# One table load at the start of a fused attention and feed-forward kernel: a set that holds both exponential and logarithm

## The chip, the cores and the metric

The kernel runs on one core of a Trainium2 chip. The metric is the device time of one execution in microseconds. Of the unchanged kernel three timed runs are there, 1183.91 to 1187.83 us with a median of 1184.35, and one more execution that the hardware profiler recorded.

The core's engines are named as in the profile: PE (TensorE, matrix products), PEld (its weight loads), DVE (VectorE), ACT (ScalarE), POOL (GpSimd) and SP (SyncE, which issues DMAs here). Each engine works through its own queue in order and waits there for what the others produce.

## The reference

Two blocks stand one behind the other. The first normalises q and k by their root mean square, takes softmax attention for 8 batches of 12 heads (448 positions, 64 wide) and hands its output, as 3584 rows of 768, to the second: a product with `w_in`, `h` times its softmax, a layer norm without bias, and a product with `w_out`.

```python
def rmsnorm(x, g):
    rms = np.sqrt(np.mean(x * x, axis=-1, keepdims=True) + 1e-06)
    return x / rms * g
q_n, k_n = rmsnorm(q, g_q), rmsnorm(k, g_k)
scores = 1.0 / np.sqrt(64) * np.matmul(q_n, k_n.transpose(0, 1, 3, 2))
attn = np.exp(scores - np.max(scores, axis=-1, keepdims=True))
attn = attn / (np.sum(attn, axis=-1, keepdims=True) + 1e-09)
x = np.matmul(attn, v).transpose(0, 2, 1, 3).reshape(3584, 768)

h = x @ w_in                                   # 768 -> 1024
e = np.exp(h - np.max(h, axis=-1, keepdims=True))
solu = h * e / (np.sum(e, axis=-1, keepdims=True) + 1e-09)
mu, var = mean and variance of solu along the row
return ((solu - mu) / np.sqrt(var + 1e-06) * g_ln) @ w_out
```

`w_in` and `w_out` arrive as 64-bit floats, the other inputs as 32-bit ones: the kernel reads the two weights as pairs of 32-bit words and builds 32-bit floats from them.

## The kernel before

The work of the attention is cut into 48 pairs of heads (`pair(n)`, lines 640 to 653). For a pair, `load` (471) brings q, k and v; there are three q/k buffers, so the load of pair n + 3 needs the buffer of pair n, which is free when `qk_transpose(n)` has read it. `norm` (482) makes the inverse root mean squares; `qk_transpose` (507) turns q and k on PE; `scores` (520), called for four chunks of k, multiplies, takes the exponential (L531) and adds up the chunks on POOL (L535); `values` (537) multiplies with v, sums the exponentials on PE into `sm`, inverts them on DVE (L557 to L559) and writes a part of `xT` (L562).

`norm` is where the logarithm is. ScalarE squares (L485), DVE sums (L488), ScalarE takes Ln (L492) and then the Exp of minus one half of it (L494), which gives a first guess of the inverse root; DVE mends it with one Newton step (L493, L495 to L497), and POOL applies it to q (L500).

The feed-forward works on 28 tiles of 128 rows: `ff_in` (574, two halves of six products into `h`), `ff_solu` (585: the maximum on DVE, the exponential at L593 on ScalarE, statistics on DVE, a power on POOL), `ff_transpose` (607) and `ff_out` (617, two halves of eight products, a copy on ScalarE, a store). Its pieces are put between the pieces of the pairs: a tile may begin when the pairs it needs are through, and at most 4 pieces go with one pair (`RATE`, lines 681 to 704). What is left at the end follows behind the last pair.

The weights are converted in 28 steps between the pieces as well (`convert_w`, 444): `w_in` spread over the first 12 pairs, `w_out` over pairs 12 to 23. A step is five instructions on DVE, two on ScalarE (L452, L454) and the product on POOL or DVE (L459, L462).

The order in which each engine's instructions stand is not the order of these calls alone: the framework's scheduler moves instructions of one queue past one another where no data forbids it. In the trace the square of the second pair, for example, stands ahead of the first pair's L494.

ScalarE's functions are Square, Copy, Relu, Ln and Exp. The program says nothing of tables; the ACT_TABLE_LOAD instructions in the trace were put in when it was compiled.

`setup` (415) is called behind the first `load` and ahead of the first `norm`; it fills constants, makes the identity and turns the gains. The kernel has a second path for large gains (`general_path`, behind a condition at L753) that these inputs don't take.

Of the kernel before, what the change touches and what calls it, by code (L numbers as in the profile page):

```python
# [366 lines left out]
def fast_path(  # L367
# [16 lines left out]
    nc = tc.nc  # L384
# [28 lines left out]
    eps = consts.tile([P, 1], FP32, name="eps")  # L413

    def setup():
        nc.gpsimd.memset(mhalf, -0.5)
        nc.gpsimd.memset(m896, -896.0)
        nc.gpsimd.memset(eps, 1e-6)
        nc.gpsimd.memset(ones, 1.0)
        make_identity(nc, ident)  # L420
        pg = ps_t.tile([P, KF + 2], FP32, tag="t", name="pg")
        nc.tensor.transpose(pg, grow, ident[0 : KF + 2, 0 : KF + 2])
        nc.vector.tensor_copy(gcol, pg)  # L423

        nc.vector.tensor_scalar(
            gcol[:, KF : KF + 1], gcol[:, KF : KF + 1], gcol[:, KF + 1 : KF + 2], within, OP.mult, OP.mult
        )
# [226 lines left out]

    load(0)
    setup()
    load(1)
    norm(0)
# [126 lines left out]
```

## Time and profile before

| | |
|---|---|
| timed runs | 1183.91, 1184.35, 1187.83 us; median 1184.35 |
| profiled execution, its own time | 1183.37 us |
| its span, first to last instruction | 1181.6 us |
| mean granted PE clock | 0.965 of full |
| busy: PE, ACT, DVE, POOL | 1062.1, 533.1, 518.3, 392.5 us |

The profile is one execution. Busy times are sums over the span, and the span has stretches of different make: attention and weight conversion first, then attention and feed-forward mixed, then feed-forward alone. A row of a group reads: line, engine, operation, how many, then busy microseconds and the mean nanoseconds of one, then the idle time of the engine ahead of them and what ended it. The chain of waits is followed back from the last instruction: each step to what released it.

### The profile page before, as it was taken

The page shows a single profiled execution, that of the slowest core. Times are in us where ns is not written, and L with a number is a line of the kernel's source. Part 1 is how long each engine was busy: PE and PEld are TensorE (multiplying, and loading weights), DVE is VectorE, ACT ScalarE, POOL GpSimd, SP SyncE. Part 2 cuts the span into 40 slices and gives each one's busy share as a digit, 9 for nine tenths or more (in the row PEclk, how much of TensorE's full clock was granted, in tenths as well). Part 3 has the DMA queues.
Part 4 walks back from the last instruction along what each step waited for, and adds up shares of the span by engine and source line. Part 5 has one row for each costly group of instructions (what it writes and reads, how often), then busy time and mean ns, then how long its engine had stood idle before and what let it go on. Part 6 is the DMA issues. An engine that isn't in the chain of part 4 may idle for free.

```text
span 1181.6 us, 10970 instructions
## 1 busy us (share of the span) xinstructions
PE 1062.1 (90%) x3905; PEld 483.6 (41%) x3905; DVE 518.3 (44%) x922; ACT 533.1 (45%) x869; POOL 392.5 (33%) x242
## 2 busy tenths in 40 slices
PE   3667887997677999999999999999999999999997
PEld 1222333342223444444444444444444444455554
DVE  3896445578777344334233434334233433311300
ACT  6666786347776654434343435433343423110111
POOL 2756656144555532223232322223232322200000
PEclk9687999999977999999999999999999999999999
DMA  6521222013332111111111111111111100000001
GB/s 179 152 62 42 67 57 75 22 49 83 94 87 74 47 53 38 37 45 37 37 37 38 44 33 37 37 45 37 38 37 37 38 1 14 14 14 26 14 28 42
DMA packets 109047, 57.50 MB, mean 49 GB/s; under 512 B 91056, under 2 KB 101816, under 8 KB 108984
## 3 DMA queue, kind: packets, MB, share of 16 engines
q1 hardware_dynamic: 104640, 45.63, 15.0%
q10 hardware_dynamic: 4344, 11.08, 2.4%
q8 instruction: 33, 0.54, 0.2%
q14 instruction: 30, 0.25, 0.1%
HBM read 45.68 MB, written 11.01 MB: 48 GB/s over the span
## 4 chain that ended last, share of the span: by engine, by line
PE 68%; DVE 11%; ACT 11%; DMA 4%; issue 2%; SPq 2%; POOL 1%; ACTq 0%; DVEq 0%; POOLq 0%
PE po L624 25%; PE h L581 23%; PE s L527 9%; PE o L547 7%; DMA qk<-in_k_dram 3%; ACT E L531 3%; PE pt L514 2%; ACT L494 2%; PE sm L553 2%; SPq L479 2%; ACT sq L485 2%; DVE rs L488 1%; PE pu L614 1%; ACT L492 1%; DVE tmp L450 1%
## 5 line engine op out<-in xcount | busy, mean ns | idle before, releaser
L531 ACT ACTIVATE E<-s,rs 112x448 f32<-112x448 f32 x384 | 221.7, 633 | 243.6 <-PE s L527 241.1
L581 PE MATMUL h<-w_in,xT 128*128 128x512 f32 x672 | 312.1, 611 | 18.5 <-DVE xT L562 13.0
L624 PE MATMUL po<-w_out,uT 128*128 128x384 f32 x896 | 301.3, 491 | 6.8 <-ACT uT L615 6.2
L535 POOL TENSOR_TENSOR es<-es,E 112x896 f32<-112x896 f32 x96 | 203.3, 2118 | 256.5 <-ACT E L531 256.1
L527 PE MATMUL s<-qkT 64*112 64x448 f32 x768 | 195.5, 609 | 29.3 <-DVE qkT L518 19.4
L624 PEld LDWEIGHTS po<-w_out,uT 128*128 128x128 f32 x896 | 166.3, 190 | 135.6 <-ACT uT L615 14.4
L581 PEld LDWEIGHTS h<-w_in,xT 128*128 128x128 f32 x672 | 124.3, 193 | 172.9 <-issue 156.5
L535 POOL TENSOR_TENSOR es<-E 112x896 f32<-112x896 f32 x48 | 101.8, 2122 | 261.6 <-ACT E L531 261.6
L547 PE MATMUL o<-E,v 112*64 112x448 f32 x768 | 161.2, 561 | 0.0
L527 PEld LDWEIGHTS s<-qkT 64*112 64x112 f32 x768 | 63.0, 184 | 146.2 <-issue 109.3
L625 ACT COPY y<-po 128x384 f32<-128x384 f32 x56 | 26.6, 476 | 200.1 <-PE po L624 200.1
L488 DVE TENSOR_REDUCE rs<-sq 112x16 f32<-112x1024 f32 x48 | 58.4, 1217 | 109.4 <-ACT sq L485 109.0
L590 DVE TENSOR_REDUCE hmax<-h 128x1 f32<-128x1024 f32 x28 | 34.2, 1222 | 162.5 <-PE h L581 162.4
L547 PEld LDWEIGHTS o<-E,v 112*64 112x64 f32 x768 | 52.6, 141 | 107.7 <-issue 89.8
L485 ACT ACTIVATE sq<-qk 112x1024 f32<-112x1024 f32 x48 | 50.7, 1057 | 79.3 <-DMA qk<-in_k_dram 79.1
L500 POOL TENSOR_TENSOR qn<-qk,rs 112x512 f32<-112x512 f32 x48 | 55.8, 1162 | 85.1 <-PE pt L514 59.7
L514 PE MATMUL pt<-ident,qn 112*128 112x112 f32 x192 | 30.4, 284 | 49.5 <-DVE r L557 17.0
L518 DVE TENSOR_SCALAR qkT<-pt,gcol 128x448 f32<-128x448 f32 x48 | 32.6, 678 | 92.0 <-PE pt L514 92.0
L557 DVE STREAM_TRANSPOSE r<-sm 128x448 f32<-128x448 f32 x48 | 30.9, 643 | 83.1 <-PE sm L553 83.1
L492 ACT ACT_TABLE_LOAD x48 | 61.6, 1283 | 4.6 <-DVE gcol L423 3.8
L494 ACT ACT_TABLE_LOAD x43 | 55.2, 1283 | 0.8
L495 DVE TENSOR_TENSOR nx<-nx,ny 112x16 f32<-112x16 f32 x48 | 18.1, 377 | 81.4 <-ACT ny L494 81.4
(57 smaller groups left out, 747.8 us busy)
## 6 DMA issues: line engine op xcount, KB each, us to landing
qk<-in_q_dram SPq DMA_DIRECT2D x96, 112.0 KB, 2.9
qk<-in_k_dram SPq DMA_DIRECT2D x96, 112.0 KB, 3.0
v<-in_v_dram SPq DMA_DIRECT2D x48, 224.0 KB, 2.6
out_dram<-y ACTq DMA_DIRECT2D x28, 384.0 KB, 2.3
raw<-in_moe_w_in_dram SPq DMA_DIRECT2D x12, 512.0 KB, 4.9
raw<-in_moe_w_out_dram SPq DMA_DIRECT2D x16, 384.0 KB, 3.2
grow<-in_g_q_dram ACTq DMA_DIRECT2D x2, 0.2 KB
grow<-in_g_k_dram ACTq DMA_DIRECT2D x2, 0.2 KB
```

The source lines that it names most:

```text
L485: nc.scalar.activation(sq, d["qk"].rearrange("p s j h d -> p (s j h) d"), AF.Square)
L488: nc.vector.tensor_reduce(flat, sq, AX, OP.add)
L492: nc.scalar.activation(y, flat, AF.Ln, scale=1.0 / D, bias=eps[0:SP])
L494: nc.scalar.activation(y, y, AF.Exp, scale=-0.5)
L500: nc.gpsimd.tensor_tensor(d["qn"], d["qk"][:, 0].rearrange("p j h d -> p (j h) d"), rs[:, 0].rearrange("p j h -> p (j h) ()").to_broadcast ...
L514: nc.tensor.transpose(pt[:, j * SP : (j + 1) * SP], src, ident[0:SP, 0:SP])
L527: nc.tensor.matmul(s, d["qkT"][hh, 1, kc * SP : (kc + 1) * SP], d["qkT"][hh, 0, :], start=True, stop=True)
L531: nc.scalar.activation(d["E"][:, kc, h], d["s", h], AF.Exp, scale=d["rs"][:, 1, kc, h : h + 1])
L535: nc.gpsimd.tensor_tensor(d["es"], d["E"][:, 0] if kc == 1 else d["es"], d["E"][:, kc], OP.add)
L547: nc.tensor.matmul(o[h * D : (h + 1) * D, :], d["v"][:, h, kc * D : (kc + 1) * D], d["E"][:, kc, h], start=(kc == 0), stop=(kc == NJ - 1),)
L581: nc.tensor.matmul(d["h"][:, hs], xTs[m][:, c, i * P : (i + 1) * P], w_in[:, c, hs], start=(c == 0), stop=(c == KD - 1))
L624: nc.tensor.matmul(po, d["uT"][:, c], w_out[:, c, hs], start=(c == 0), stop=(c == KF - 1))
```

## The change

One instruction is added at the head of `setup`: a load of the activation table set with number 6, which holds both the exponential and the logarithm. Nothing else in the program is changed; where other loads stand is, as before, decided when it is compiled.

```diff
@@ -413,6 +413,12 @@
     eps = consts.tile([P, 1], FP32, name="eps")
 
     def setup():
+
+        nc.scalar.add_instruction(
+            mybir.InstLoadActFuncSet(
+                act_func_set_id=6, name=nc.get_next_instruction_name(), engine=mybir.EngineType.Activation
+            )
+        )
         nc.gpsimd.memset(mhalf, -0.5)
         nc.gpsimd.memset(m896, -896.0)
         nc.gpsimd.memset(eps, 1e-6)
```

## The prediction

> **What bounds the kernel now.** I read the page's totals first, then ScalarE's instructions grouped by line, then busy time by stretch of the span, then the waits and the chain that ended last, and at the end one turn of that chain in order of time.
>
> ```profile
> span 1181.6 us, 10970 instructions
> PE 1062.1 (90%) x3905; PEld 483.6 (41%) x3905; DVE 518.3 (44%) x922; ACT 533.1 (45%) x869; POOL 392.5 (33%) x242
> L492 ACT ACT_TABLE_LOAD x48 | 61.6, 1283 | 4.6 <-DVE gcol L423 3.8
> L494 ACT ACT_TABLE_LOAD x43 | 55.2, 1283 | 0.8
> ...
> L531 ACT ACT_TABLE_LOAD x5 | 6.4, 1283 | 0.1
> L485 ACT ACT_TABLE_LOAD x1 | 1.3, 1283 | 5.3 <-DMA qk<-in_k_dram 5.3
> ```
>
> TensorE (PE) is busy 90% of the span, ScalarE (ACT) 45%. ScalarE loads a table 48 + 43 + 5 + 1 = 97 times, 1.283 us each: 124.5 us (61.6 + 55.2 + 6.4 + 1.3), 23% of its busy time. One load stands before each of the 48 Ln (L492) and one before what follows it, the Exp of L494 or, 5 times, the scores' Exp of L531. Whether those 124.5 us set the time depends on the stretch:
>
> ```profile
> core 0: us, PE busy (x) PEld busy (x) DVE busy (x) ACT busy (x) POOL busy (x), PEclk, DMA share, GB/s
> 0.00:25.00 25.00, 6.98 (x23) 3.56 (x23) 8.37 (x26) 15.80 (x21) 4.01 (x13) 1.00 0.64 148
> 25.00:105.00 80.00, 49.14 (x185) 18.75 (x184) 68.56 (x103) 55.64 (x91) 54.95 (x31) 0.77 0.37 108
> 105.00:203.00 98.00, 78.60 (x378) 31.84 (x378) 42.24 (x88) 72.42 (x116) 58.26 (x33) 0.97 0.25 62
> 203.00:250.00 47.00, 44.19 (x124) 18.12 (x124) 30.37 (x55) 18.92 (x31) 13.97 (x10) 0.96 0.14 38
> 250.00:400.00 150.00, 117.74 (x496) 46.19 (x496) 109.21 (x192) 101.22 (x169) 77.62 (x42) 0.89 0.30 78
> 400.00:450.00 50.00, 48.59 (x186) 22.56 (x184) 18.79 (x34) 26.43 (x42) 15.17 (x10) 1.00 0.15 44
> 450.00:1026.00 576.00, 570.41 (x2060) 262.16 (x2058) 209.80 (x373) 223.84 (x370) 163.72 (x101) 1.00 0.12 34
> ```
>
> From 450 us on PE is busy 570.41 of 576.00 us: what ScalarE does there is hidden, and after 1026 us there are no loads. Before 400 us PE has gaps, and there the loads can count. The chain that ended last holds 30 whole loads between these two, the first and the last of them, and none behind 450 us:
>
> ```profile
> 13.95 1.28 ACT L494
> ...
> 426.89 1.28 ACT L494
> ```
>
> By stretch the 30 are 4 before 25 us, 6 from 25 to 105, 11 from 105 to 203, none from 203 to 250, 7 from 250 to 400 and 2 from 400 to 450. One turn of the chain, out of the steady part of the third stretch (start, duration, engine, line; in brackets the idle time before):
>
> ```profile
> 159.69 1.06 ACT L485 ACTIVATE sq<-qk 112x1024 f32<-112x1024 f32 x1
> 160.76 1.28 ACT L492 ACT_TABLE_LOAD   x1
> 160.84 1.22 DVE L488 TENSOR_REDUCE rs<-sq 112x16 f32<-112x1024 f32 x1 [4.70 <-ACT sq L485]
> 161.89 1.76 PE L527 MATMUL s<-qkT 64*112 64x448 f32 x8
> 162.10 0.31 ACT L492 ACTIVATE ny<-rs,eps 112x16 f32<-112x16 f32 x1
> 162.42 1.28 ACT L494 ACT_TABLE_LOAD   x1
> 163.72 0.21 ACT L494 ACTIVATE ny<-ny 112x16 f32<-112x16 f32 x1
> 163.84 2.19 ACT L531 ACTIVATE E<-s,rs 112x448 f32<-112x448 f32 x4
> 163.96 0.18 DVE L495 TENSOR_TENSOR nx<-nx,ny 112x16 f32<-112x16 f32 x1 [1.69 <-ACT ny L494]
> 164.06 0.64 DVE L557 STREAM_TRANSPOSE r<-sm 128x448 f32<-128x448 f32 x1
> 164.75 0.60 PE L514 MATMUL pt<-ident,qn 112*128 112x112 f32 x4 [1.10 <-DVE nx L496]
> 165.89 1.23 SPq L479 DMA_DIRECT2D qk<-in_q_dram  x2
> 167.16 1.28 SPq L479 DMA_DIRECT2D qk<-in_k_dram  x2
> 171.40 1.06 ACT L485 ACTIVATE sq<-qk 112x1024 f32<-112x1024 f32 x1 [0.74 <-DMA qk<-in_k_dram]
> ```
>
> This is a loop of 171.40 - 159.69 = 11.71 us per pair: square, sum on VectorE (DVE), Ln, load, Exp, then DVE's queue (L495 waits for Exp, and L557, which reads the `sm` bank so that PE can have it back, stands behind L495), the transposes, the four DMA issues that reuse the q/k buffer, their landing, the next square. Two loads stand in it, and they are not worth the same.
>
> **The change part by part.** *One load added in setup.* It stands on ScalarE behind the DMA issues of lines 740 to 745 and replaces the load at L485:
>
> ```profile
> 5.25 1.28 ACT L485 ACT_TABLE_LOAD   x1 [5.25 <-DMA qk<-in_k_dram]
> ...
> 9.46 0.23 DVE L747 TENSOR_TENSOR gg<-gg 128x64 f32<-128x64 f32 x1 [9.46 <-DMA gg<-in_g_k_dram]
> ...
> 10.11 1.20 DVE L488 TENSOR_REDUCE rs<-sq 112x16 f32<-112x1024 f32 x1
> ```
>
> The first square ends at 5.25 + 1.28 + 1.06 = 7.6 us, but its reader on DVE starts at 10.11, since it is queued behind L747 and the gains' DMA. The load has 2.5 us of cover wherever it lands: 0, from -1.3 to +1.3 without the cover. Nothing but ScalarE's own square is queued behind it.
>
> *48 loads before Ln removed.* In the turn above that load runs 160.76 to 162.04 while DVE reduces the squares from 160.84 to 162.06, and Ln needs that sum. Without the load Ln still starts at 162.1: worth 162.10 - 162.06, nothing. The reduction is what hides it. Where the sum is ready before, the load counts in full; that is so in the first 25 us, and in few turns later.
>
> *48 loads before the Exp (43 at L494, 5 at L531) removed.* Nothing covers these for DVE: it stands 1.69 us in the turn above, the load's 1.28 and Exp's 0.21 among it. How much of such waiting there is, by stretch (0 to 25, 25 to 105, 105 to 203, 250 to 400, 450 to 1030 us):
>
> ```profile
> DVE nx L495 <- ACT ny L494: 4.2, 3, 2.5
> ...
> L495 DVE TENSOR_TENSOR nx<-nx,ny 112x16 f32<-112x16 f32 x5 | 1.9, 382 | 2.5 <-ACT ny L494 2.5
> ...
> DVE nx L495 <- ACT ny L494: 13.6, 8, 1.7
> ...
> DVE nx L495 <- ACT ny L494: 7.8, 7, 1.7
> ...
> DVE nx L495 <- ACT ny L494: 45.1, 18, 3.2
> ```
>
> The sum, stretch by stretch:
>
> - 0 to 25: the 4 chain loads are 5.1 us. Without them the next limit is the second pair's square and reduction, 1.06 + 1.22, and the first pair's transposes, so not all comes back. I take 3.4, two thirds; bounds 2.0 and 5.1.
> - 25 to 105: DVE is busy 68.56 of 80 us with converting the weights; it waits for Exp only 2.5 us. I take those 2.5; bounds 0 (the conversion takes up the slack) and 6 x 1.283 = 7.7.
> - 105 to 203: 8 turns wait 1.7 us each, 1.28 of it load. What is late next: the transposes could start at 164.75 - 1.28 = 163.47, but PE is in the scores until 161.89 + 1.76 = 163.65, so a turn saves 164.75 - 163.65 = 1.10. 8 x 1.10 = 8.8; bounds 6.4 (0.8 a turn, if each refilled q/k landing also slips by some tenths, as the 0.74 us of waiting before the last row does) and 8 x 1.283 = 10.3.
> - 203 to 250: PE busy 44.19 of 47, no load on the chain: 0; bounds 0 and 1.
> - 250 to 400: 7 waits of 7.8 us together, 6 of the chain's 7 loads stand at L494. I take 5.0, about two thirds of the waits, because DVE is busy 109.21 of 150 and has conversion work that is queued in the same order; bounds 1.5 and 7.8.
> - 400 to 450: PE idles 1.4 us in all: 0.7; bounds 0 and 1.4.
> - 450 on: DVE's 45.1 us of waiting for Exp is under PE at 99%: 0; bounds 0 and 2 (of PE's 5.6 idle us).
>
> Together 3.4 + 2.5 + 8.8 + 0 + 5.0 + 0.7 + 0 = 20.4 us; the low bounds give 9.9, the high ones 35.3, and all 30 chain loads at full length 38.5. The profiled execution took 1183.37 us (its span of 1181.6 and 1.8 around it), so 1163.0 for a like one; it lies 1.0 below the median of the runs, 1184.35. I predict 1163.5.
>
> On the price of a load. In the turn above the Ln ends at 162.41, the load runs 162.42 to 163.70, the Exp starts at 163.72: a load stands the engine 1.28 us and a few hundredths. The Trainium skill ("ScalarE: Activation LUTs", What ACT_TABLE_LOAD costs) puts about 1380 ns of drain beside those 1283 ns, 2.66 us for each switch; by that the sum would be about twice as large. This case's rows do not show such a drain around the small Ln and Exp.
>
> **The rivals.**
>
> 1. *The loads go and everything on the chain follows.* Ln's loads turn out to count too, because earlier Exps pull the sums forward, and PE, whose granted clock is 0.77 and 0.89 in the stretches with gaps, is fed better. All 30 chain loads: 38.5 us, 1145.5. For it: 10 of the chain's 30 loads stand at L492. Against: in the steady turns the reduction takes Ln's load over almost to the hundredth. A drain of the skill's size, which the rows deny, would land here or a few us lower.
> 2. *Only the long loop pays.* The conversion stretches absorb their part, since DVE is busy 86% and 73% there: 8.8 from the third stretch alone, near 1175.
> 3. *The loads stay.* If whatever placed one load before each Ln and one behind it places by function and not by what the tables hold, the new load is a 98th and covered: 1184. For it: 97 loads stand although a set with both functions exists, as the change has it. Against: Square, Copy and Relu run between them with no load of their own (the groups have loads at L492, L494 and L531, and one at L485), so what is loaded is kept track of. The Trainium skill ("ScalarE activation tables: per-element evaluation and per-set limits", Table sets in the compiler and the runtime) says that loads are placed by the set that serves the longest run of activations. By that rule the shared set would have served the whole run already and the change would move nothing; the 97 loads show that this program wasn't placed so.
> 4. *Slower: the scores' Exps move in between Ln and Exp.* ScalarE's order is written for loads that cost 1.28 us; 5 times a group of L531 already stands between the two (the loads at L531). If with the loads gone four scores' Exps, 2.19 us, stand there in every turn, the loop grows by 2.19 - 1.28 = 0.91: 8 x 0.91 = 7.3 in the third stretch, and 9 turns with 0.91 in the fifth, 8.2, less the 3.4 of the start: 1184.4 + 12.1 = 1196. It decides from three scores' Exps on (2.19 / 4 = 0.55 us each, three of them over 1.28). Against it: 43 of 48 have nothing in between.
>
> **How the numbers follow.** The forecast 0.62, with its own range 1153 to 1172; everything follows (1) 0.13; only the loop (2) 0.13; the loads stay (3) 0.05; slower (4) 0.07. A measurement of this kernel can't tell less than 0.3%, 3.6 us, from no change. Faster is then 0.62 + 0.13 + 0.13 = 0.88, same 0.05, slower 0.07. The range goes from 1147, which takes in most of the first rival and the sum's high bounds (1149), to 1176, which takes in the second and almost the low bounds (1174.5); what is left out, 3, 4 and the tip of 1, is about 0.16.
>
> **What would show it.** ACT_TABLE_LOAD falls from 97 to one or two, ScalarE's busy time by about 123 us to some 410. DVE's wait for `ny` at L495 falls in the third stretch from 1.7 to about 0.4 a turn, the turn shown from 11.71 to near 10.6, and Ln now shows an idle time of about 1.2 us that the sum at L488 ends. Everything behind 450 us keeps its length and only starts 20 us earlier. The forecast is wrong if the loads are still counted by the dozen, if ScalarE's order between Ln and Exp is another, or if the stretch with conversions ends as late as before.

## The result, and the profile after

The changed kernel takes 1159.2 us (median of 4 runs, 1158.07 to 1159.22) against 1184.62 for the kernel before (median of 4 runs, 1183.91 to 1187.83): a ratio of 0.9778, with a 95% interval from 0.9759 to 0.9797. That is 26.3 us less (24.0 to 28.5); 1163.5 was forecast. The added lines move the numbers of all later lines up by 6: L498 is the Ln, L500 the Exp behind it, L501 DVE's wait for it, L520 the transposes.

From the page of the changed kernel:

```profile
span 1157.4 us, 10878 instructions
PE 1058.2 (91%) x3905; PEld 483.1 (42%) x3905; DVE 516.4 (45%) x922; ACT 410.9 (35%) x773; POOL 394.2 (34%) x242
```

and three rows of its ScalarE instructions grouped by line:

```profile
L498 ACT ACTIVATE ny<-rs,eps 112x16 f32<-112x16 f32 x48 | 14.9, 310 | 44.2 <-DVE rs L494 44.1
L500 ACT ACTIVATE ny<-ny 112x16 f32<-112x16 f32 x48 | 10.4, 217 | 1.3
L417 ACT ACT_TABLE_LOAD x1 | 1.3, 1283 | 4.3 <-DMA qk<-in_q_dram 4.3
```

One load is left of 97, and ScalarE's busy time fell from 533.1 to 410.9 us, by 122.2; 96 x 1.283 are 123.2. Only a fifth of it, 24.2 us of span, came off the end. ScalarE now stands idle 44.1 us ahead of Ln, 0.92 us each time, for the sum on DVE beside which the loads used to run.

Busy time by stretch, the stretches cut at the same work as before (the span starts a little differently from one execution to the next, so the ends are good to about 2 us):

```profile
0.00:20.00 20.00, 7.92 (x27) 4.24 (x28) 7.43 (x22) 8.93 (x17) 3.81 (x13) 1.00 0.74 189
20.00:99.00 79.00, 48.58 (x190) 19.05 (x188) 70.99 (x104) 42.29 (x77) 58.04 (x31) 0.78 0.37 111
99.00:185.00 86.00, 76.92 (x370) 30.69 (x371) 44.90 (x93) 53.72 (x102) 57.36 (x33) 0.97 0.27 68
185.00:231.00 46.00, 43.66 (x122) 18.12 (x124) 30.45 (x53) 12.79 (x26) 13.50 (x10) 0.96 0.16 42
231.00:377.00 146.00, 115.70 (x498) 45.72 (x496) 107.22 (x192) 78.68 (x151) 77.79 (x42) 0.89 0.31 80
377.00:426.00 49.00, 49.00 (x188) 22.73 (x186) 18.77 (x34) 18.69 (x36) 15.61 (x10) 1.00 0.16 45
426.00:1002.00 576.00, 570.40 (x2062) 262.24 (x2060) 206.19 (x373) 177.43 (x335) 163.45 (x102) 1.00 0.12 34
```

The third stretch shrank from 98 to 86 us, the fifth from 150 to 146, and the long one, 576 us with PE busy 570.40, is the same to the tenth. ScalarE has 46 us less to do in it, and that is worth nothing.

A turn of the third stretch in the changed kernel, in order of time:

```profile
147.31 1.06 ACT L491 ACTIVATE sq<-qk 112x1024 f32<-112x1024 f32 x1 [0.21 <-DMA qk<-in_k_dram]
148.47 1.22 DVE L494 TENSOR_REDUCE rs<-sq 112x16 f32<-112x1024 f32 x1 [4.79 <-ACT sq L491]
149.42 1.76 PE L533 MATMUL s<-qkT 64*112 64x448 f32 x8
149.72 0.31 ACT L498 ACTIVATE ny<-rs,eps 112x16 f32<-112x16 f32 x1 [1.36 <-DVE rs L494]
150.06 0.22 ACT L500 ACTIVATE ny<-ny 112x16 f32<-112x16 f32 x1
150.31 0.18 DVE L501 TENSOR_TENSOR nx<-nx,ny 112x16 f32<-112x16 f32 x1 [0.41 <-ACT ny L500]
150.97 0.13 DVE L502 TENSOR_TENSOR nx<-nx,ny 112x16 f32<-112x16 f32 x1
151.12 0.60 PE L520 MATMUL pt<-ident,qn 112*128 112x112 f32 x4
...
153.67 1.76 PE L533 MATMUL s<-qkT 64*112 64x448 f32 x8 [0.69 <-DVE qkT L524]
157.08 1.06 ACT L491 ACTIVATE sq<-qk 112x1024 f32<-112x1024 f32 x1
```

DVE's wait at L501 is 0.41 us where it was 1.69. The transposes start at once behind the scores (149.42 + 1.76 = 151.18) where PE stood idle 1.10 us, and from square to square are 9.77 us where 11.71 were. The two turns shown are extremes, though: the six turns from pair 6 to pair 12 take 11.37 us on average before and 10.03 after. In the turn shown PE works 9.08 of 9.77 us and waits 0.69 us, for `qkT`. It does not close every turn: the chain that ended last still goes through the landing of k in four turns of this stretch, for 12.5 us of its 86 (start and duration):

```profile
113.83 3.09 DMA qk<-in_k_dram
...
134.13 3.24 DMA qk<-in_k_dram
...
144.33 2.88 DMA qk<-in_k_dram
...
164.04 3.24 DMA qk<-in_k_dram
```

Where the time came off is best seen at one instruction that every pair has, ScalarE's copy of k's transposes into `qkT`. The table gives how much earlier it starts than in the kernel before (there 19.5, 107.0, 203.4, 262.4, 395.1, 462.9 and 994.7 us), from the time-ordered rows of each kernel's profile:

| kernel | pair 0 | 5 | 13 | 15 | 24 | 27 | 47 |
|---|---|---|---|---|---|---|---|
| changed | 6.0 | 6.5 | 18.5 | 18.5 | 23.0 | 24.5 | 24.5 |
| the same, second profile (e7) | 4.1 | 4.6 | 16.4 | 16.4 | 23.9 | 25.5 | 25.5 |
| changed, one `y` buffer (e9) | 3.5 | 4.0 | 15.8 | 17.5 | 23.2 | 24.7 | 24.7 |
| old order, one load (e1) | 0.9 | 3.6 | 14.6 | 16.3 | 21.1 | 22.6 | 22.6 |
| the same, second profile (e8) | 1.5 | 3.6 | 15.5 | 15.5 | 21.3 | 22.9 | 22.9 |
| new order, all loads (e2) | 1.4 | -4.6 | -1.1 | -1.1 | -1.2 | -0.8 | -0.8 |
| changed, loads at Ln (e3) | 4.2 | 2.3 | 14.5 | 16.2 | 21.4 | 22.9 | 22.9 |
| changed, loads at Exp (e4) | 2.7 | 1.4 | 4.5 | 4.6 | 5.0 | 3.9 | 3.9 |
| changed, 32 late loads (e5) | 4.1 | 4.6 | 16.4 | 16.4 | 21.0 | 22.6 | 22.6 |
| before, four q/k buffers (e10) | -0.4 | -0.7 | 14.4 | 15.8 | 9.0 | 10.7 | 10.6 |
| changed, four q/k buffers (e6) | 4.1 | 11.7 | 25.4 | 27.2 | 31.8 | 34.1 | 34.1 |
| the same, second profile (e11) | 3.9 | 11.6 | 23.9 | 25.7 | 30.1 | 32.4 | 32.4 |

From pair 27 to pair 47 every row stands still to within 0.1 us. Before that two profiles of the same work differ by 2 to 3 us (the first two rows; and e5, which is the changed kernel up to pair 32, is 2.9 us behind e7 at pair 24). A row is good to so much, and the timed ratios decide.

The length of a steady turn varies less, by 0.2 us between profiles of one program. These are the four turns from pair 8 to pair 12, from one such copy to the next, on average:

| kernel | us a turn |
|---|---|
| before | 11.42 |
| new order, all loads (e2) | 10.91 |
| changed, loads at Exp (e4) | 11.04 |
| changed, loads at Ln (e3) | 9.83 |
| old order, one load (e1, e8) | 9.88, 9.80 |
| changed (first profile, e7, e5, e9) | 9.96, 9.77, 10.00, 9.97 |
| before, four q/k buffers (e10) | 9.33 |
| changed, four q/k buffers (e6, e11) | 9.35, 9.32 |

### The profile page after: what moved, and what is told of

The parts are those of the page before. It is cut to its first block, busy times and chain, and to the rows that moved or that the text cites. A ratio compares the mean times of both kernels' runs of the same rounds, so it can differ in the third digit from the quotient of the medians.

```text
span 1157.4 us, 10878 instructions
## 1 busy us (share of the span) xinstructions
PE 1058.2 (91%) x3905; PEld 483.1 (42%) x3905; DVE 516.4 (45%) x922; ACT 410.9 (35%) x773; POOL 394.2 (34%) x242
## 4 chain that ended last, share of the span: by engine, by line
PE 73%; DVE 12%; ACT 6%; DMA 4%; issue 3%; POOL 1%; SPq 1%; ACTq 0%; POOLq 0%; DVEq 0%
PE po L630 26%; PE h L587 24%; PE s L533 10%; PE o L553 8%; ACT E L537 2%; PE sm L559 2%; DMA qk<-in_k_dram 2%; PE pt L520 2%; DMA raw<-in_moe_w_out_dram 1%; PE pu L620 1%; DVE tmp L456 1%; DVE rs L494 1%; DVE tmp L463 1%; SPq L485 1%; DVE xT L568 1%
## 5 line engine op out<-in xcount | busy, mean ns | idle before, releaser
L491 ACT ACTIVATE sq<-qk 112x1024 f32<-112x1024 f32 x48 | 50.7, 1057 | 80.5 <-DMA qk<-in_k_dram 80.3
L520 PE MATMUL pt<-ident,qn 112*128 112x112 f32 x192 | 30.4, 284 | 34.0 <-DVE r L563 9.4
L610 POOL TENSOR_TENSOR he<-he,mhalf 128x1 f32<-128x1 f32 x28 | 15.6, 557 | 107.8 <-DVE he L609 107.4
L568 DVE TENSOR_TENSOR xT<-o,r 128x448 f32<-128x448 f32 x48 | 46.4, 970 | 4.9 <-PE h L587 3.7
L520 PEld LDWEIGHTS pt<-ident,qn 112*128 112x128 f32 x192 | 20.0, 147 | 65.2 <-DVE r L563 11.6
```

The costliest lines, as they stand in the source:

```text
L491: nc.scalar.activation(sq, d["qk"].rearrange("p s j h d -> p (s j h) d"), AF.Square)
L520: nc.tensor.transpose(pt[:, j * SP : (j + 1) * SP], src, ident[0:SP, 0:SP])
L568: nc.vector.tensor_tensor(xTs[b // 2][:, hp, c0 : c0 + S].rearrange("d (p j) -> d j p", j=NJ), o.rearrange("d (j p) -> d j p", j=NJ), r.re ...
```

## The experiments

**Loads or order?** The change does two things. It takes 96 loads away, and the scheduler, which now has one instruction more to place, wrote another order: PE's instructions stand as before, but on ScalarE, DVE, POOL and SP the first 115 us or so are rearranged (behind them every engine's order is the same, the loads aside). The prediction had the second only as a rival, and only for the worse. Two kernels part them. In the one the program is the kernel before, and one load is put into ScalarE's finished queue, so the old order stands and no other load is needed; in the other the changed kernel's load is taken out of its finished queue, so the new order stands and the loads come back.

```diff
--- before.py, behind the scheduling
+    ahead of ScalarE's first activation: mybir.InstLoadActFuncSet(act_func_set_id=6, ...)
--- after.py, behind the scheduling
-    the mybir.InstLoadActFuncSet of setup
```

Expected of the first:

> Every engine works in the order of the kernel before, but the table set with both functions is loaded once, at the start, and the other 96 loads are gone. Theory A (the loads alone make the gain; that the instructions of the first 100 us also came into another order when the load was added is without effect): 1159, as the changed kernel, within 2 us. Theory B (the loads give what the prediction summed, 20.4 us, and the rest of the 25.4 us comes from the new order of the first 100 us): 1163 to 1166, with the difference to the changed kernel made before pair 5 and none behind it.

Measured: 1161.17 us, ratio 0.9814 (0.9797 to 0.983). That is 2 us under theory B and 0.2 outside theory A: nearly the whole gain comes with the loads alone. Expected of the second:

> Every engine works in the order of the changed kernel, but the single load is taken out again, so that the loads stand function by function as before (97 of them). Theory A: 1184.6 as the kernel before, within 2 us. Theory B: 1179 to 1182, since the new order of the first 100 us keeps some 3 to 5 us. Under both the loads cost 18 us behind pair 5.

Measured: 1185.25 us, ratio 1.0022 (1.0013 to 1.0032). So theory B's number for this one fell: the new order keeps nothing when the loads are back, it costs 2.6 us (0.0022 x 1183; 1.5 to 3.8 by the interval). To see what it is worth without them, the changed kernel and the first of the two ran side by side on one chip:

> The changed kernel once more, beside the others on one chip, so that they are compared without a difference between chips: ratio to the kernel before 0.976 to 0.980. Theory that the new order of the first 100 us is worth something without the loads: 1.5 to 3 us less than the kernel in the old order without loads.

> The kernel in the order of before with one load at the start, once more beside the changed kernel. Theory that order and loads go together (the old order suits the loads, the new one their absence): 1.5 to 3 us above the changed kernel, all of it from before 250 us. Theory that the order does nothing: within 0.5 us of it.

Measured: 1158.62 us, ratio 0.9794 (0.9778 to 0.9811), and 1160.02 us, ratio 0.98 (0.9784 to 0.9816). The intervals lie on one another: 1.4 us between the medians point to the new order, which is just under what the one theory expected and over what the other did, and they are not resolved. What is shown is that the loads make the gain: 22 to 24 us in the old order (0.0186 and 0.02 of 1183, in two comparisons) and some 27 in the new one (1.0022 against 0.9794). With the loads in, the old order is the better one, by those 2.6 us. Why the scheduler wrote another one was not looked into.

**Which of the two loads?** The changed kernel, with a needless load of the same set put back into the finished queue ahead of every Ln, or ahead of every Exp behind it:

```diff
+    ahead of each activation of L498 (Ln):  mybir.InstLoadActFuncSet(act_func_set_id=6, ...)     (e3)
+    ahead of each activation of L500 (Exp): mybir.InstLoadActFuncSet(act_func_set_id=6, ...)     (e4)
```

> The changed kernel with one needless load of the same set put straight ahead of each of the 48 Ln. Theory of the prediction (these loads are covered by the sum on VectorE, 1.22 us against 1.28): 1159 to 1162. Rival (a load counts wherever it stands on the chain; 10 of the 30 loads on the chain before stood at Ln, 12.8 us): 1169 to 1173.

Measured: 1161.32 us, ratio 0.9819 (0.9802 to 0.9836).

> The changed kernel with one needless load of the same set put straight ahead of each of the 48 Exp behind Ln. Theory of the prediction (nothing covers these): 9 to 10 us in the eight turns of the third stretch, 4 to 6 between pairs 15 and 26, 1 to 3 before pair 5: 1173 to 1178. Rival (the two kinds of load are worth the same, half of 25.4 each): 1170 to 1173, and the kernel with loads at Ln as much. If the sequencer drained the engine for a further 1.4 us at a load, as the Trainium skill (ScalarE: Activation LUTs, What ACT_TABLE_LOAD costs) states, it would be above 1185.

Measured: 1177.73 us, ratio 0.995 (0.9933 to 0.9967). Against the changed kernel's 0.9794 the loads at Ln cost 3.0 us (0.0025 x 1183; the intervals overlap), those at Exp 18.5 (against its first measurement, 0.9778, 4.9 and 20.3). Both times lie where the prediction's theory had them, and the rival that both kinds are worth the same fell.

The two prices don't add up to the 27 us of both together. Where Exp's loads stand, those at Ln cost 7.5 us more (e2 against e4, 1185.25 - 1177.73), and the table has 6.0 of it before pair 5 (-4.6 against 1.4). So the loads at Ln are covered in the steady turns, and not at the start.

The loads put in here carry no line of the program and have no row of their own; they are seen as idle time in front of the Exp, in e4's group of that line (the lines that put the loads in move the numbers by another 22: L520 is the Ln, L522 the Exp, L525 DVE's wait for it):

```profile
L522 ACT ACTIVATE ny<-ny 112x16 f32<-112x16 f32 x48 | 10.4, 216 | 63.0 <-issue 63.0
```

63.0 us for 48 loads are 1.31 us each, all in. In the changed kernel the same line has 1.3 us of idle time in all. And DVE waits again as it did before, in e4's third stretch:

```profile
DVE nx L525 <- ACT ny L522: 13.5, 8, 1.7
```

In the table, pairs 5 to 13: the changed kernel gains 12.0 us there, with loads at Exp 3.1, with loads at Ln 12.2. Eight loads at Exp cost 8.9 us, 1.1 a turn; eight at Ln cost nothing. With both (e2) the gain is 3.5, as with Exp's alone. These are the two sizes the prediction had worked out for the turn. By place e4's loads cost 3.2 to 5.1 us before pair 5 and 6.6 to 9.7 between pairs 13 and 27, against the two profiles of the changed kernel; 1 to 3 and 4 to 6 were expected. Its profiled execution, at 1179.51 us, lies 1.8 above its median.

**Is PE's cover whole?** 32 needless loads, ahead of Ln and Exp of the last 16 pairs alone (e5):

```diff
+    ahead of the Ln and the Exp of pairs 32 to 47: mybir.InstLoadActFuncSet(act_func_set_id=6, ...)
```

> The changed kernel with needless loads put ahead of Ln and of Exp for the last 16 pairs alone (32 loads, 41 us of ScalarE's time, all in the stretch where TensorE is busy 99%). Theory of the prediction (TensorE covers them all): within 0.5 us of the changed kernel. Rival (VectorE's 45 us of waiting for Exp there counts in part): 5 to 20 us above it.

Measured: 1159.41 us, ratio 0.979 (0.9771 to 0.9809), 0.8 us over the changed kernel beside it with intervals that overlap. The profile is sharper: from pair 27 to pair 47 its row in the table moves by less than 0.1 us, although DVE waits nearly as long as it did before the change (45.1 us behind 450). The stretch from 450 to 1000 us in e5, and then in the changed kernel, by waits:

```profile
DVE nx L525 <- ACT ny L522: 41.6, 17, 3.4
```

```profile
DVE nx L501 <- ACT ny L500: 5.6, 13, 0.5
```

That is 36 us more of waiting on DVE, and the end doesn't move: here the wait of an engine that isn't the bound costs nothing.

**What closes the turn now?** The third stretch gained more than was forecast for it, and the landing of q and k stands in the same loop as the loads. With four q/k buffers a pair's load needn't wait for the transposes of the pair three ahead; to make room, `y` has one buffer (e6).

```diff
-        d["qk"] = loads.tile([SP, 2, NJ, 2, D], FP32, tag="qk", name="qk", bufs=3)
+        d["qk"] = loads.tile([SP, 2, NJ, 2, D], FP32, tag="qk", name="qk", bufs=4)
-            d["y"] = work.tile([P, DM], FP32, tag="y", name="y")
+            d["y"] = work.tile([P, DM], FP32, tag="y", name="y", bufs=1)
```

> The changed kernel with four q/k buffers in place of three (and one y buffer in place of two, to make room), so that a pair's load no longer needs the transposes of the pair three ahead of it. Theory A (with the loads gone TensorE's own turn of some 9.9 us sets the third stretch, and the landing is off the loop but for a few tenths): 1 to 3 us less than the changed kernel. Theory B (the landing still closes the loop, as it did before): a turn falls to 9 us, 6 to 10 us less. The new buffer changes the order the scheduler writes, so some us either way are that.

Measured: 1150.46 us, ratio 0.9725 (0.9706 to 0.9744). The time is theory B's, and so is the steady turn, 9.35 us where it was 9.8 to 10.0. But the table has most of the 8.2 us ahead of pair 5: from pair 5 to 7 this kernel is slower than the changed one, and that takes back what the turns behind it gain. Three more kernels part it: the `y` buffer alone (e9), the same buffers in the kernel before (e10), and this one again beside them (e11).

> The changed kernel with one y buffer in place of two and three q/k buffers as it had; every engine's order stays. It parts the two edits of the kernel with four q/k buffers. Theory that its gain of some 8 us comes from the q/k buffer: as the changed kernel, within 1 us, 1157 to 1160. Rival (the y buffer or the place of the tiles does it): 1150 to 1153.

Measured: 1158.53 us, ratio 0.9789 (0.9772 to 0.9805): the `y` buffer does nothing, the q/k buffer does it, with the order that the scheduler writes for it.

> The kernel before, with all its loads, with four q/k buffers and one y buffer. Theory A (buffer and loads are separate costs): about 8 us under the kernel before, 1174 to 1177. Theory B (with the loads ScalarE's own turn binds, so that the early landing is worth little): 1179 to 1184. Theory C (with the loads the landing closed the loop of the third stretch, so that the buffer is worth more here than without them): 1168 to 1172.

Measured: 1170.91 us, ratio 0.989 (0.9874 to 0.9907): 13.0 us, theory C.

> The changed kernel with four q/k buffers and one y buffer once more, beside the two kernels that part its edits: ratio to the kernel before 0.970 to 0.975.

Measured: 1150.97 us, ratio 0.9721 (0.9705 to 0.9737).

Read with the turns: taking the loads away shortens the steady turn from 11.42 us to 9.8 to 10.0, the buffer alone to 9.33, and both together to 9.32 to 9.35. Once the buffer is there the loads are worth nothing in these turns; once the loads are gone the buffer still brings some 0.5 us. That fits the loop of the prediction: load and landing are two of its links. With four buffers the chain that ended last holds neither a landing of q and k nor a load in these turns, in either kernel, and PE works some 9.15 us of each, less than the 9.9 that theory A gave it. With the loads alone gone the landing is still on it. But four buffers come with another order: ScalarE's and DVE's instructions are rearranged at over a hundred places each, up to some 930 us. Buffer and order were not parted.

ScalarE's waits for the landing, in the kernel before with four buffers and in the changed one with four, by groups of ScalarE (with three buffers the two kernels had 79.1 and 80.3 us):

```profile
L485 ACT ACTIVATE sq<-qk 112x1024 f32<-112x1024 f32 x48 | 50.7, 1056 | 16.5 <-DMA qk<-in_k_dram 16.5
```

```profile
L491 ACT ACTIVATE sq<-qk 112x1024 f32<-112x1024 f32 x48 | 50.7, 1055 | 45.8 <-DMA qk<-in_k_dram 45.5 <-issue 0.2
```

What the buffer gives on top of the change comes for the most part before pair 5 (11.6 against 4 to 6.5 us). In the kernel before with four buffers 21 of its 48 loads behind Ln stand at the scores' Exp where 5 did, and pairs 15 to 24 lose 6.8 us.

```profile
L494 ACT ACT_TABLE_LOAD x27 | 34.6, 1283 | 0.5
L531 ACT ACT_TABLE_LOAD x21 | 26.9, 1283 | 1.3 <-PE s L527 0.9
```

That is the mechanism of the prediction's fourth rival, here with the loads present: the order is seen, that it causes those 6.8 us is only inferred. The changed kernel with four q/k buffers is the fastest of all that ran, 1150 to 1151 us.

## Why the prediction was right, point by point

- **Removed and added loads.** 97 went to 1, 122 us of ScalarE, and the added load is covered: it ends at 5.6 us and the first square waits for its data until 6.93. As forecast.
- **Loads at Ln worth nothing.** Right for the turns of the third stretch, where the sum covers them (e3). All 48 cost 3.0 us by themselves and 7.5 us where Exp's loads stand too, most of it before pair 5: the prediction let them count at the start, and did not say how much.
- **Loads at Exp.** Right in place and size in the third stretch: 1.10 a turn was worked out from the transposes that run into PE's scores, and e4 gives 8.9 / 8 = 1.1.
- **The sum by stretch.** 20.4 us were summed. In the order that the prediction assumed, 22 to 24 came (22.6 and 22.9 in the profiles e1 and e8); in the new order 24 to 26 (24.5 to 25.5 in the profiles of the changed kernel, e7 and e9).
  - Up to pair 5 the forecast was 3.4 and 2.5. The first square starts up to 2.5 us later in these profiles than in the kernel before, so the gain is counted from there: the old order gains 2.6 to 3.4 us up to pair 0 and 2.1 to 2.7 from there to pair 5, as forecast. In the new order the split is another, 5.2 to 6.4 and 0.5.
  - From pair 5 to 13 it was 8.8 against 11.1 and 11.9 in the old order and 11.8 to 12.0 in the new. This is the term that was mis-sized: it took the saving worked out from one turn eight times. The excess isn't the price of Exp's loads, since e4 and e2, which have them, are 3.1 and 3.5 us quicker there than the kernel before too. Of this 1.4 to 1.5 us are in the turn from pair 5 to 6, and 1.3 to 1.6 in the two turns from pair 10 to 12. In those two the landing of k takes 3.55 and 3.32 us on the chain of the kernel before, against 2.60 to 3.07 wherever it stands on e2's in this stretch; the turn shown in the prediction ends with the first of them. Why these landings took longer, and why the first and the last of the eight turns gain more than 1.1, stays open.
  - From pair 13 to 27 5.7 were forecast and 6.0 to 9.1 came. Behind it 0 were forecast and 0 came.
- **The order.** The prediction took the order as given except in its fourth rival, and there only for the worse. That the scheduler plans again when a load is added was the unseen step; the runs put its effect at -1.4 us (not resolved) without loads and +2.6 us with them. That it is so small is luck: nothing in the prediction bounded it.
- **The rivals.** That everything follows (1145.5) fell by e3: the Ln loads hardly count in the steady turns. That only the loop pays (1175) fell: the other stretches gave about half. That the loads stay fell at once. The slower case didn't come: scores' Exps stand between Ln and Exp at 6 of the 48 places, where 5 were before.
- **The price of a load.** In the prediction's turn a load starts 0.01 us behind the Ln and the Exp 0.02 us behind the load. e4's loads, of the set that is in already, take 1.31 us each (63.0 / 48). The 2.66 us for a switch that the Trainium skill gives ("ScalarE: Activation LUTs", What ACT_TABLE_LOAD costs) are not borne out by either.

The forecast of 1163.5 stands 4.3 us over the measured 1159.2, and the range of 1147 to 1176 holds it.

## What to carry to other kernels

Sum an instruction's busy time only over the stretches where it is on the chain, and there by what covers it: here 123 us of removed loads were worth 24 to 26. The 48 that run beside a reduction cost 3 us when put back alone, the 48 that nothing runs beside 18.5, and those of 16 pairs under a full TensorE nothing that shows. A link that is taken out of a loop pays only down to the next loop, so two links of one loop (a table load, a landing) are not added up. A saving that is multiplied by a number of turns should be read from more than one of them. And where a scheduler writes the order, an added or removed instruction can rewrite it elsewhere: part the two by editing the finished queue.

## What the runs showed of the hardware

A DVE operation on 112x16 elements lasts as long here as one on 112x896 on POOL. In the changed kernel with four q/k buffers (e6) DVE's busy time rose from 516.4 to 572.6 us with the same 922 instructions. In order of time, POOL and DVE:

```profile
142.78 2.08 POOL L541 TENSOR_TENSOR es<-E 112x896 f32<-112x896 f32 x1
142.89 2.01 DVE L502 TENSOR_TENSOR nx<-nx,ny 112x16 f32<-112x16 f32 x1
```

The L502 that took 0.13 us in the turn of the changed kernel takes 2.01 here and ends 0.04 us behind POOL's addition. The Trainium skill ("SBUF — State Buffer", section "SBUF: two separate sides") says that the two engines share a port pair which the one that starts first holds for its whole instruction, among others against a DVE operation with two inputs in SBUF; these rows agree with it. In the second profile of this kernel (e11) L501 and L502 stand on the chain that ended last, at about 1.9 and 2.0 us in each of the steady turns; those take 9.32 us all the same, as in the kernel before with four buffers (e10). Moving the Newton step away from POOL's additions was not tried.

The start of an execution varies: the first square, which waits for the first q and k to land, starts at 6.93 us in the changed kernel's profile and at 8.54 in the second profile of the same program (e7), so that differences of up to 2 us at pair 0 need not come from a change.
